# Chunk 0 of a delta-rule chain feeding a GELU MLP: masked Gram products from the plain Gram matrix, loads on two queues, a new order for the early part

## The chip, the cores and the metric

The kernel runs on one core of a Trainium2 chip. The metric is the device time of one execution in microseconds; runs of one kernel are summed up by their median. The profile is one further execution, recorded instruction by instruction.

## What is computed

The reference runs a delta-rule recurrence per batch and head (4 x 8 heads, 768 tokens, 48 numbers a head), lays the heads of a token side by side (3072 tokens x 384), and puts the result through an MLP with 2048 hidden features:

```python
k_n = k / (np.linalg.norm(k, axis=-1, keepdims=True) + 1e-06)
for t in range(S):
    y[:, :, t] = q_t @ state
    state = state + beta_t * outer(k_n_t, v_t - k_n_t @ state)
x = y.transpose(0, 2, 1, 3).reshape(B * S, H * D)
h = x @ w_in                                   # 384 -> 2048
out = gelu_tanh(h) @ w_out                     # 2048 -> 384
```

## The kernel before

The sequence is cut into 12 chunks of 64 tokens (`c` = 0 to 11). A chunk has two units (`u = 2c + x`) of 8 head slots on 128 partitions. All steps are added as named operations, and one text, `ORDER`, lists them in the order in which each engine takes them: `name:a` is ScalarE (ACT), `:d` VectorE (DVE), `:g` GpSimd (POOL), `:s` SyncE (SP), a name without a letter is TensorE (PE), and `@n` is the PSUM bank. Semaphore waits come from the reads and writes of the operations. Each engine works through its own list strictly in order, and a load is an entry of the list of the queue that issues it.

For each chunk the steps are these.

- `k c.ay`, `q`, `v`: loads of 96 KB each (chunk 0's keys in eight quarters `k0x0`, `k0x1` of 48 KB), into three slots a tensor. `sq`, `sum`, `pow`, `eps`, `inv`, `kn`: the keys are normalised; `qb`, `vb` convert queries and values.
- `T` or `Tk`, `Tq`, then `kT`, `kTk`, `kTq`: transposes on PE and the copies out of PSUM. `G` or `GD`, `GQ`: Gram matrices, copied by `dn` (keys with keys) and `wq` (keys with queries).
- The leaf: `F` gathers the 8 x 8 diagonal blocks, `lp`, `x0`, `L` and six pairs `xm`, `xa` on DVE solve them row by row; `xb` multiplies by beta and `xe` spreads the result into the block-diagonal tile `zt`.
- `KZ` multiplies the keys by `zt` on PE, `kz` copies the negative out as the third part of `kT`, and `GM` forms from it the products of the remaining inverse, which `lw` writes under a mask into the tile `lw`. `X10`, `X11` build the start, `A4`, `rt4`, `B4`, `bde4` (or `xi4`, `bdc4`), `A5`, `rt5`, `B5`, `be5` double the inverted blocks to 64.
- The chain: `V`, `K`, `R`, `U`, `Un`, `S`, `Sn` carry the state; `Q`, `O`, `On` give the chunk's output; `X` and `xT` transpose it on PE (or `turnx` by a DMA transpose).
- The MLP: sixteen `up` of three matmuls, four `gelu` on ACT, eight `down` of four matmuls, and copies and stores `Z`, `out`.

The two halves of the first weight matrix (`w1.0`, `w1.1`, 768 KB each) are issued by POOL. They are declared as readers of the slot of chunk 1's keys, so that they start after those keys:

```python
A(("pool",), f"w1.{i}", lambda e, P, f0=f0: e.dma_start(W1[:, :, f0:f0 + FF // 2], w1v[:, :, f0:f0 + FF // 2]),
  reads=["kraw10", "kraw11"], writes=[f"W1{i}"], dma=f"w1{i}")
```

The keys of chunk 4 go into that slot, so every `k4` load waits until both halves have landed. `w2` and the slot of chunk 0's values stand in the same way, and hold back `v3`.

`fill` operations are matmuls of a zero tile `wz` (128 x 128 by 128 x 512) that nothing reads; 140 are declared and the order of before uses two.

Of the kernel before, what the change touches and what calls it, by code (L numbers as in the profile page):

```python
# [8 lines left out]
ALU = mybir.AluOpType  # L9
# [3 lines left out]
C = 64  # L13
# [16 lines left out]
mwp1:g dn.5:a GM.1@4 xec.1:d KZ.0@0 ladj5.0:a F.2@3 wqa.5:a betaC3:a lw.1:d kz.0:a lp.2:d bdz1:d L.2@3 k3.01:s GM.0@4 x0.2:d X10.1:g KZ.2@6 lw.0:d  # L30
KZ.3@0 kz.3:a X11.1:g kz.2:a xm1.2:d GM.3@0 xa1.2:d rpad1:g A4.1@2 X11.0:g lw.3:d X10.0:g rt4.1:d k3.10:s xm2.2:d A4.0@1 X11.3:g xa2.2:d v1.01:s
B4.1@2 xm3.2:d xa3.2:d rt4.0:d q3.11:s GQ.2@6 GM.2@4 vb.0:a xm4.2:d vb.1:g wq.2:d k4.11:s B4.0@1 bde40.1:a triwq3:g lw.2:d V.0@6 X10.3:g k4.01:s
bde41.1:a bde40.0:a k4.00:s wqb.1:g xa4.2:d A4.3@2 xm5.2:d bde41.0:a A5.1@0 k4.10:s rt4.3:d GQ.3@4 R.0:a rt5.1:d A5.0@1 X11.2:g B4.3@2 v1.10:s rt5.0:d
B5.1@0 bde40.3:a xa5.2:d q3.00:s B5.0@7 X10.2:g xm6.2:d fill115@1 xa6.2:d be50.1:d be50.0:a v1.11:s wq.3:d xb.2:g be51.1:a A4.2@3 sq.3:a w2.0:g
be51.0:d v2.01:s xe.4:d U.0@0 bde41.3:d KZ.4@4 Un.0:a w2.1:g rt4.2:d kz.4:a O.0@6 sum.3:d A5.3@4 On.0:a S.0@2 rt5.3:d GM.4@0 sq.4:a xe.5:d X.0@6
B4.2@7 lw.4:d Sn.0:a fill85@4 KZ.5@4 xT.0:a sum.4:d X11.4:g bde40.2:a up4.0@2 kz.5:d pow.3:g up0.0@0 bde41.2:a up1.0 X10.4:d tabG:a up2.0 up12.0@6
qbc.3:d up3.0 A5.2@4 up13.0 rt5.2:d gelu0.0:a up5.0 up6.0 GM.5@4 eps.3:d inv.3:d knc.3:d up7.0 up14.0 A4.4@0 lw.5:d up15.0 turn.7:s B5.2@1 gelu3.0:a
rt4.4:d up8.0@4 X11.5:g up9.0 gelu1.0:a B5.3@0 vbc.1:g down00.0@6 be50.3:d up10.0 be51.3:a X10.5:d pow.4:g be50.2:a up11.0 V.1@2 gelu2.0:a T.6@0
v2.00:s A4.5@7 kT.6:d v2.10:s be51.2:a K.1 down01.0 R.1:a rt4.5:d q5.00:s G.6@4 k5.10:s B4.5@7 dn.6:a B4.4@2 xi4.5:d U.1@0 bde40.4:a down02.0 k5.00:s
wq.6:d bdc40.5:g Un.1:a down03.0 k5.01:s bde41.4:d bdc41.5:g eps.4:g A5.5@1 k5.11:s Z0.0:d wqb.5:g S.1@4 Q.1@2 q4.11:s Sn.1:d G.7@6 O.1 vbc.2:g  # L40
q4.01:s A5.4@0 rt5.5:d On.1:a down10.0@5 inv.4:d q4.10:s dn.7:d kn.9:g down11.0 rt5.4:d q4.00:s wq.7:d F.3@1 q5.01:s B5.4@4 lp.3:d V.2@2 sq.5:a x0.3:d
# [73 lines left out]
class Flow:  # L115
# [74 lines left out]
    def emit(self, nc, psum):  # L190
        count, total, names = {e: 0 for e in self.queues}, {}, list(self.queues)
        for e in self.queues:
            for o in self.queues[e]:
                if o.dma is None:
                    count[e] += 1
                    o.tag = (e, count[e])
                else:
                    if o.dma not in total:
                        total[o.dma] = 0
                        names.append(o.dma)  # L200
                    total[o.dma] += 16
                    o.tag = (o.dma, total[o.dma])
# [56 lines left out]
def bass_deltanet__then__act_gelu_tanh_kernel(  # L259
# [16 lines left out]
    LB = 8  # L276
# [627 lines left out]
```

## Time and profile before

| what | value |
|---|---|
| median of 3 runs | 255.12 us (253.94 to 255.86) |
| profiled execution, first to last instruction | 254.7 us |
| time of the profiled execution outside its span | not given by the page; the median is 0.42 us above the span |
| TensorE busy | 226.0 us, 89% |
| VectorE busy | 185.8 us, 73% |
| ScalarE busy | 157.4 us, 62% |
| GpSimd busy | 130.1 us, 51% |

Shares of busy time are taken over the whole span; the part before the first `up` and the part after it differ, so the profile is read stage by stage. In a row of a group or of a timeline, the line number is that of the operation or of a helper that records it (L343 and L349 are the copy and the negation that many steps use). In the table by stretches, each engine has its busy time in us and the number of its instructions, then come the granted TensorE clock (1.00 is full), the mean share of the DMA engines and GB/s.

### The profile page before, as it was taken

Reading aid. Unit: us, or ns where it says so; the run is one execution under the profiler, and the core shown is the slowest. Engines: PE = TensorE matmul, PEld = TensorE weight load, DVE = VectorE, ACT = ScalarE, POOL = GpSimd, SP = SyncE. Lnnn points to the kernel's source line nnn. Section 1 sums busy time; section 2 is a strip of 40 time slices with the busy share of each in tenths; the row PEclk is TensorE's granted clock in tenths of the full one; section 3 lists DMA queues with packets and bytes.
Section 4 is the critical chain, followed back from the end, with each engine's and each line's share of the span. In section 5 each row is a group of like instructions: output and inputs, shape, how many; then the busy total and the mean of one; then the engine's idle time right before and its main releaser. Section 6 shows DMA issues by size and latency. Waiting matters only on the chain.

```text
span 254.7 us, 12256 instructions
## 1 busy us (share of the span) xinstructions
PE 226.0 (89%) x5500; PEld 178.3 (70%) x5502; DVE 185.8 (73%) x445; ACT 157.4 (62%) x244; POOL 130.1 (51%) x159
## 2 busy tenths in 40 slices
PE   0259558899999998999999899999999999999994
PEld 0148347687877877777778778787786778678672
DVE  6599989955996989898888779898494665755100
ACT  2637747949568888967647577743866534436261
POOL 7647448347563397627358968472535525330000
PEclk9999956689999999999999999999999999999999
DMA  5986995987785679789678517787359320332042
GB/s 103 165 144 118 184 162 95 165 127 117 128 130 105 112 126 124 135 165 147 119 146 167 100 36 131 147 153 130 56 93 167 62 49 4 33 68 64 3 93 62
DMA packets 104532, 28.25 MB, mean 111 GB/s; under 512 B 98592, under 2 KB 103712, under 8 KB 104480
## 3 DMA queue, kind: packets, MB, share of 16 engines
q1 hardware_dynamic: 99200, 23.79, 54.0%
q0 software_dynamic: 2880, 3.15, 7.8%
q8 instruction: 43, 0.70, 1.2%
q10 hardware_dynamic: 2400, 0.54, 1.1%
q14 instruction: 9, 0.07, 0.1%
HBM read 20.64 MB, written 4.72 MB: 100 GB/s over the span
## 4 chain that ended last, share of the span: by engine, by line
PE 73%; DVE 15%; ACT 4%; DMA 2%; ACTq 2%; issue 2%; SPq 1%; POOL 0%
PE ps L835 24%; PE ps L824 22%; PE ps L692 5%; PE ps L620 3%; PE ps L752 3%; PE ps L773 2%; DMA vraw<-in_v_dram 2%; PE ps L697 2%; PE ps L564 2%; DVE lw L623 2%; DVE xl L658 2%; PE ps L633 2%; PE ps L759 2%; DVE ps L655 2%; PE ps L609 1%
## 5 line engine op out<-in xcount | busy, mean ns | idle before, releaser
L824 PE MATMUL ps<-xT,W 128*128 128x256 bf16 x576 | 76.8, 277 | 0.4 <-DVE xl L658 0.4
L835 PE MATMUL ps<-W,gT 128*128 128x384 bf16 x384 | 72.7, 326 | 0.0
L828 ACT ACTIVATE gT<-ps 128x1024 bf16<-128x1024 f32 x48 | 48.4, 1022 | 26.4 <-PE ps L824 25.8
L824 PEld LDWEIGHTS ps<-xT,W 128*128 128x128 bf16 x576 | 52.2, 99 | 9.3 <-DVE xl L658 0.5
L835 PEld LDWEIGHTS ps<-W,gT 128*128 128x128 bf16 x384 | 34.0, 97 | 18.2
L682 POOL TENSOR_SCALAR_AFFINE_SELECT bd<-lw 64x512 bf16<-64x512 bf16 x34 | 22.6, 667 | 37.7 <-DVE lw L623 28.6
L704 DVE TENSOR_TENSOR rl<-ps,two 128x384 bf16<-128x384 f32 (+1 forms) x48 | 22.9, 484 | 9.7 <-PE ps L692 9.5
L623 DVE CAST_PREDICATED lw<-mlw,ps 128x832 bf16<-128x832 uint16 x24 | 24.3, 1018 | 6.8 <-PE ps L620 6.5
L499 POOL TENSOR_TENSOR nrm<-nrm,half 128x16 f32<-128x16 f32 x9 | 26.6, 2956 | 2.8 <-DVE nrm L497 2.7
L343 ACT ACTIVATE bd<-ps 32x256 bf16<-32x256 f32 (+1 forms) x40 | 16.8, 428 | 8.2 <-PE ps L692 4.4
L692 PEld LDWEIGHTS ps<-lw,bd 128*128 128x128 bf16 x384 | 15.5, 98 | 4.2 <-POOL bd L682 1.2
L692 PE MATMUL ps<-lw,bd 128*128 128x32 bf16 (+1 forms) x384 | 17.2, 183 | 1.2 <-POOL bd L682 1.1
L658 DVE TENSOR_TENSOR xl<-ps,xl 128x96 bf16<-128x96 f32 (+4 forms) x72 | 16.0, 228 | 2.0
L655 DVE TENSOR_TENSOR ps<-ps,xl 128x64 f32<-128x64 f32 (+5 forms) x72 | 15.6, 221 | 2.0 <-PE ps L649 0.5
L343 ACT ACTIVATE ob<-ps 128x384 f32<-128x384 f32 x17 | 8.3, 490 | 14.0 <-PE ps L835 14.0
L722 POOL COPY bd<-xi 64x256 f32<-64x256 f32 x20 | 8.0, 401 | 16.4 <-ACT xi L343 8.5
L540 PE MATMUL ps<-ident,tok 128*128 128x128 bf16 x80 | 7.8, 246 | 8.1 <-POOL tok L531 3.8
L531 POOL TENSOR_TENSOR tok<-kraw,nrm 128x384 bf16<-128x384 f32 x9 | 8.5, 945 | 12.7 <-DVE bsb L349 5.6
L349 ACT ACTIVATE kT<-ps 128x512 bf16<-128x512 f32 x18 | 10.4, 596 | 6.4 <-PE ps L609 6.4
L343 ACT ACTIVATE dn<-ps 128x512 bf16<-128x512 f32 x18 | 10.4, 593 | 5.3 <-PE ps L564 5.3
L620 PE MATMUL ps<-kT 48*64 48x56 bf16 (+1 forms) x768 | 11.1, 196 | 2.8 <-ACT kT L349 1.4
L599 POOL TENSOR_TENSOR zt<-xb,blk 128x2048 bf16<-128x2048 bf16 x3 | 10.9, 3642 | 4.1 <-DVE xb L669 3.9
(132 smaller groups left out, 428.3 us busy)
## 6 DMA issues: line engine op xcount, KB each, us to landing
qraw<-in_q_dram SPq DMA_DIRECT2D x48, 96.0 KB, 3.6
vraw<-in_v_dram SPq DMA_DIRECT2D x48, 96.0 KB, 3.5
kraw<-in_k_dram SPq DMA_DIRECT2D x44, 96.0 KB, 3.6
out_dram<-ob SPq DMA_DIRECT2D x22, 192.0 KB, 3.0
W<-in_moe_w_in_dram POOLq DMA_DIRECT2D x2, 768.0 KB, 8.8
W<-in_moe_w_out_dram POOLq DMA_DIRECT2D x2, 768.0 KB, 9.6
kraw<-in_k_dram ACTq DMA_DIRECT2D x7, 48.0 KB, 3.3
out_dram<-ob SPq DMA_DIRECT2D x3, 96.0 KB, 2.2
```

The costliest lines, as they stand in the source:

```text
L343: return e.activation(out, in_, ACT.Copy) if e is nc.scalar else e.tensor_copy(out, in_)
L499: if e is nc.scalar else e.tensor_tensor(nr[:, 1, hx], nr[:, 0, hx], half[:, hx], ALU.pow), reads=[nrn, "half"] + ["one"] * (c < ROOTS),
L620: ins = e.matmul(P(ps("GM"))[hf(a), o_ + c0:o_ + c1], kT[s][r, y, g, hf(a)], kT[s][r, z, g, C * a + c0:C * a + c1])
L623: A(("dve",), op("lw"), lambda e, P: e.copy_predicated(lw[m][:, :, 0:LW - LB], mlw[:, :, :].rearrange("p w t -> p (w t)")[:, 16:16 + LW - ...
L655: A(("dve",), f"xm{m}.{c}", lambda e, P, m=m, w=w, part=part: e.tensor_tensor(part(P), P(f"L.{c}")[:, off[m]:off[m] + 2 * H * w].rearrange ...
L658: A(("dve",), f"xa{m}.{c}", lambda e, P, m=m, part=part: e.tensor_tensor(xl[y][:, :, m + 1:LB], part(P), xl[y][:, :, m + 1:LB], ALU.add), ...
L682: A(("pool", "dve"), op(f"X1{a}"), lambda e, P, src=lw[m][hf(a), :, LW - C:LW], dst=bd[b_][hf(a), :, hf(a)], a=a: e.affine_select(out=dst, ...
L692: ins = e.matmul(P(name)[:, C * h + c0:C * h + c1], bd[b_][:, h, :], rhs[:, h, :])
L704: A(("dve",), op(f"rt{i}"), lambda e, P, i=i, c0=c0, c1=c1, r_=r_: e.tensor_tensor(r_[:, 0:H, c0:c1], P(ps(f"A{i}")).rearrange("p (h t) -> ...
L824: ins = e.matmul(P(ph)[:, 256 * f:256 * f + 256].rearrange("p (x t) -> p x t", x=2), W1[:, j, 128 * (i + f):128 * (i + f) + 128], x_[:, :, ...
L828: A(("act",), f"gelu{i // 4}.{c}", lambda e, P, i=i, ph=ph: e.activation(g_[:, i:i + 4, :], P(ph).rearrange("p (f t) -> p f t", f=4), ACT. ...
L835: ins = e.matmul(P(po)[:, 0:DM], g_[:, f, 128 * b:128 * b + 128], W2[:, f, :], start=(f == 0), stop=(f == FC - 1))
```

## The change

Four things are changed; what the kernel computes stays the same.

1. For chunk 0 alone, `KZ` and `kz` go. `GM` is formed straight from `dn`, the Gram matrix that is copied anyway, and `zt`. The sign that `kz` gave is put into `xb.0`, and taken out again where `R.0` copies.
2. Every load may be issued from SP or ACT. ACT issues 25 of them instead of 7, all before the unchanged part of its list; the stores may go on either queue, and in the text all but one (`out01.11`) stay on SP, as before.
3. Semaphore counts of DMAs are given in the order of the text rather than queue by queue, since one tensor's loads may now be issued from two queues.
4. `ORDER` is new up to the middle of chunk 1's MLP. From `up3.1` on PE (and from `qb.11` on DVE, `gelu0.1` on ACT, `pow.5` on POOL, `turn.9` on SP) each engine's list is that of before, with other PSUM banks.

Up to `up3.1` PE's list loses `KZ.0`, `KZ.1` and `X.1` (chunk 1 is transposed by `turnx.1`, a DMA, instead) and has 37 fills in place of two. The fills come in runs of one to six between the early steps. `GM.4`, `B4.2` and `KZ.5` stood ahead of the first `up` and now stand behind it; the first `up` is now `up8.0` instead of `up4.0`. `On.0` goes from ACT to DVE, `X10.1`, `X11.1`, `X10.0` from POOL to DVE, `dn.2` and `dn.3` from ACT to DVE. On ACT the words around one load are now

```
wqa.1:a q3.01:a q5.11:a kz.3:a dn.5:a vbc.0:a dn.4:a wqa.4:a wqa.5:a k4.11:a kz.2:a bde40.1:a bde41.1:a triwq3:a xi4.0:a R.0:a
```

and POOL's list around the weights is `kn.0 trilw0 triwq1 rpad0 sq.2 mln0 mwp0 w1.0 mln1 eps.2 triwq2 pad5 mwp1 qb.4 w1.1`.

The diff without the order text:

```diff
-        for e in self.queues:
-            for o in self.queues[e]:
-                if o.dma is None:
-                    count[e] += 1
-                    o.tag = (e, count[e])
...
+        for o in self.queue:
+            if o.dma is None:
+                count[o.on] += 1
+                o.tag = (o.on, count[o.on])
...
-                            A(("sp", "act") if c == 0 and n == "k" else SP, f"{n}{c}" + ("" if x is None else f"x{x}") + f".{a}{y}",
+                            A(("sp", "act"), f"{n}{c}" + ("" if x is None else f"x{x}") + f".{a}{y}",
...
+            def direct(e, P):
+                for g in range(4):
+                    for p, a in quad:
+                        h, o_ = 4 * p + g, 512 * p + 2 * C * g
+                        e.matmul(P(ps("GM"))[hf(a), o_ + LW - C:o_ + LW - LB], zt[m][hf(a), h, hf(a)], d_[hf(a), h, 0:C - LB])
+                        ins = e.matmul(P(ps("GM"))[hf(a), o_:o_ + C - 16], d_[hf(a), h, :], zt[m][hf(a), h, C * a + 16:C * a + C])
+                return ins
+            if not c:
+                d_ = dn[0][:, H * x:H * x + H, :]
+                A(PE, op("GM"), direct, reads=[f"dn0{x}", f"zt{m}"], alloc=(ps("GM"), 2), mode="t", mm=32)
+            else:
... (keys, KZ, kz and gram as before)
-            A(("dve", "pool"), f"xb.{c}", lambda e, P: e.tensor_tensor(xb[y][:, :, :], xl[y][:, :, :], bc[:, c, :, :], ALU.mult),
+            A(("dve",) if c == 0 else ("dve", "pool"), f"xb.{c}", lambda e, P: e.scalar_tensor_tensor(xb[y][:, :, :], xl[y][:, :, :], -1.0, bc[:, c, :, :], op0=ALU.mult, op1=ALU.mult) if c == 0 else
+              e.tensor_tensor(xb[y][:, :, :], xl[y][:, :, :], bc[:, c, :, :], ALU.mult),
...
-            A(EV, op("R"), lambda e, P: copy(e, rb[...], banks(P(ps("K")))), frees=[ps("K")], writes=[rbn])
+            A(EV, op("R"), lambda e, P: (neg if first else copy)(e, rb[...], banks(P(ps("K")))), frees=[ps("K")], writes=[rbn])
...
-                        A(SP, f"out{a}{a}.{c}", lambda e, P, a=a, o_=o_: e.dma_start(
+                        A(("sp", "act"), f"out{a}{a}.{c}", lambda e, P, a=a, o_=o_: e.dma_start(
```

212 lines of the change are left out of this document (107 added, 105 removed).

## The prediction

> **What bounds the kernel now.** I read the page first, for the span and the shape over time, and then cut the span into stages with the table by stretches.
>
> ```profile
> span 254.7 us, 12256 instructions
> PEclk9999956689999999999999999999999999999999
> ```
>
> ```profile
> 0.00:15.00 15.00, 2.06 (x16) 1.70 (x16) 9.66 (x27) 6.53 (x11) 11.14 (x33) 1.00 0.78 136
> 15.00:44.65 29.65, 21.10 (x606) 17.97 (x607) 27.69 (x86) 18.92 (x36) 16.34 (x28) 0.83 0.82 140
> 44.65:49.94 5.29, 4.26 (x167) 3.68 (x168) 5.27 (x8) 5.03 (x8) 1.53 (x3) 0.68 1.11 160
> 49.94:75.45 25.51, 25.29 (x613) 20.19 (x606) 19.30 (x44) 16.68 (x26) 15.86 (x14) 0.93 0.84 132
> 75.45:254.70 179.25, 173.28 (x4109) 134.73 (x4107) 123.92 (x283) 110.18 (x166) 85.23 (x84) 1.00 0.56 99
> ```
>
> PE is the bound from the first `up` at 49.94 to the end: 25.29 of 25.51 us, then 173.28 of 179.25. The last row is the part whose lists are kept, from the end of `up3.1`. Before the MLP it is DVE: 27.69 of 29.65 us from 15.00 to 44.65, where its last early step, `be51.0`, releases `U.0`. So the change can move two things: when the first `up` starts, and what PE needs from there to `up3.1`. What follows shifts as a block. The chain of waits shows the link between the two stages, and the PEclk line shows a half clock just there.
>
> ```profile
> 44.22 0.43 DVE bd L343
> 45.30 0.81 ACT us L343
> 50.01 3.74 PE ps L824 x18
> 53.94 0.99 PE ps L824 x9
> 54.93 0.37 PE ps L620 x32
> 56.06 0.20 PE ps L692 x8
> ```
>
> The first six `up` take 3.74 us for 18 matmuls, the next three 0.99 for 9.
>
> **Term 1, DVE ahead of U.0.** The removed Gram step (`KZ`, `kz`) stands on PE and ACT, beside a DVE that has other work. What counts is DVE's list up to the step that releases `U.0`; both texts have 111 entries there. The groups up to 50 us and two lines of the timeline give the prices.
>
> ```profile
> L602 DVE TENSOR_TENSOR zt<-xb,blk 128x1024 bf16<-128x1024 bf16 x4 | 2.7, 702 | 0.1
> L571 DVE CAST_PREDICATED wq<-muq,ps 128x512 bf16<-128x512 uint16 x4 | 2.7, 674 | 0.0
> L343 DVE COPY kT<-ps 128x512 bf16<-128x512 bf16 x6 | 2.3, 416 | 0.3 <-PE ps L540 0.2
> L421 DVE MEMSET bd<- 128x512 f32 x4 | 1.9, 485 | 1.1 <-PEq L889 1.0
> L599 DVE TENSOR_TENSOR zt<-xb,blk 128x2048 bf16<-128x2048 bf16 x1 | 1.2, 1210 | 0.0
> L418 DVE TENSOR_SCALAR rl<-tmpl 128x256 bf16<-128x256 bf16 x1 | 0.9, 904 | 0.0
> L343 DVE CAST bd<-ps 32x256 bf16<-32x256 f32 x2 | 0.8, 410 | 0.0
> L658 DVE TENSOR_TENSOR xl<-ps,xl 128x48 bf16<-128x48 f32 x3 | 0.7, 225 | 0.0
> L346 DVE TENSOR_SCALAR bd<-ps,low 128x512 bf16<-128x512 f32 x1 | 0.7, 746 | 0.0
> ```
>
> ```profile
> 13.06 1.96 DVE L531 TENSOR_TENSOR tok<-kraw,nrm 128x384 bf16<-128x384 f32 x1
> 14.95 0.54 DVE L531 TENSOR_TENSOR tok<-kraw,nrm 128x384 bf16<-128x384 f32 x1
> 12.63 2.05 POOL L382 TENSOR_SCALAR_AFFINE_SELECT rows<-rows 128x1024 bf16<-128x1024 bf16 x1
> ```
>
> Gone from the list: `xec.1` 1.21, `wq.3` and `wq.4` 1.35, two `kTk` 0.83, two presets (`trilw0`, `triwq1`, priced as the memset of 485 ns) 1.0, `ladj5.1` and `ladj4.1` 0.9, `be50.1` and `be51.0` 0.82, five leaf steps of chunk 1's successor 1.0 (0.2 each), and some six small ones 0.8: 7.9 us. New: `xe.3` 0.70, `dn.2` and `dn.3` 1.4 (nearest row: 0.746 for 512 numbers out of PSUM), three `X1` 1.2 (0.41 as the casts of half width), `kn.1` and `sq.0b` 1.1 (0.54 each), `kTq.2` and `be51.1` 0.83, two memsets, `trilw1` and `triwq0` 2.0, `ladj5.0` 0.45, `qb.1`, `bdc40.0` and four small ones 1.1: 8.8 us. Balance +0.9. Against it stands one stall. `kn.2` took 1.96 us beside POOL's 2.05 us `rows1`, its twin 0.54; `rows1` now stands before any `kn`, so 1.4 us go. Term 1 is -0.5 us, if DVE waits as long as before (5.3 us up to 15.00, 2.0 after).
>
> That is the unknown. No row shows the waits of the new order. Below, the 5.3 us could halve, since chunk 0's keys are now issued first: -2.7. Above, new waits appear. `betaN000` and `qb.1` are placed on DVE behind loads that are the tenth on ACT and the twentieth on SP, and `xe.3` waits for a POOL `xb.1`. I allow +2. I take zero, by this row:
>
> ```profile
> 10.00:20.00 10.00, 4.74 (x90) 3.80 (x91) 9.01 (x24) 4.87 (x11) 5.11 (x9) 1.00 0.86 152
> L472 SPq DMA_DIRECT2D kraw<-in_k_dram x13: 634/637/2834, 0.8 to 25.6; - x13
> ```
>
> The DMA engines were 0.86 busy with 152 GB/s, and one queue at 96 KB per 0.64 us offers 150. A second queue can reorder the data, but hardly bring more of it. The Trainium skill says as much in "DMA: Bandwidth & Descriptors", section "Issuing engines are not separate DMA queues": loads from several engines run on the same 16 DMA engines, and only the issue time is saved. The trace agrees (0.86 at 152 GB/s); by it, the second queue alone would be worth nothing, and the sum would be the same. On ACT each issue costs about 0.6 us of its list, and twelve stand among steps that others wait for; I count them inside the +2.
>
> **Term 2, from U.0 to the first up.** Before, 5.29 us. In the rows below, `KZ.5` waited 0.36 us for DVE ahead of the first `up`; it moves behind it: -0.35. `X.0` at half clock took 0.82 us, a later `X` at full 0.50: -0.3. `U.0` shrinks alike: -0.1. `On.0` goes from ACT to DVE, behind `sum.3`; ACT took 0.81 for 768 numbers (its `Un` in the chain), DVE 0.746 for 512: +0.2. Term 2 is -0.55, bounds -1 and +1. The first `up` comes at 48.9.
>
> ```profile
> 49.58 0.43 PE L609 MATMUL ps<-zt,tok 64*64 64x64 bf16 x16 [0.36 <-DVE lw L623]
> 47.97 0.82 PE L807 MATMUL ps<-ident,xo 128*128 128x128 bf16 x6
> 68.50 0.50 PE L807 MATMUL ps<-ident,xo 128*128 128x128 bf16 x6
> 33.00:43.00 10.00, 7.53 (x255) 6.78 (x256) 8.97 (x24) 5.20 (x10) 7.29 (x12) 0.50 0.68 117
> 30.00:34.00 4.00, 1.74 (x78) 1.42 (x78) 3.94 (x7) 2.85 (x6) 0.29 (x1) 0.86 1.29 189
> 46.60:53.50 6.90, 6.49 (x123) 5.24 (x122) 4.95 (x8) 5.51 (x9) 3.61 (x2) 0.51 1.27 193
> ```
>
> **Term 3, the clock.** PE ran at half from 33 to 43 us and from 46.6 to 53.5. It fell after a stretch with 1.74 of 4 us busy. From 30 us on the new text puts 19 fills among the early steps. A fill streams 512 columns; at the `up` rate of 0.11 us for 256 (0.99 / 9) one is 0.22 us at full clock, so they add 4.2 us in some 18, a quarter of the time. I take the clock as full at the first `up`: 3.74 becomes 1.98, -1.75. If it is not, zero; below zero nothing, as the 18 matmuls then take what they took. The fills' price ahead of the MLP is hidden by PE's idle time (8.55 us of 29.65); placed in front of a step that others wait for, one costs 0.22 to 0.42, inside the +2 above. The Trainium skill, "TensorE: Matmul & The Clock Gate", section "What's actually happening", lets the clock fall after an idle window of about 3.4 us. Here it fell with PE 43% busy, so sparse work is enough; by the page alone the fills would have nothing to prevent, and the term would be the same only because the half clock was measured.
>
> **Term 4, PE from the first up to up3.1.** Three groups now stand behind the first `up`: `GM.4` 0.37, `B4.2` 0.20 and `KZ.5`, as half of the 0.43 at half clock, 0.22. Two fills add 0.44. `X.1` goes, 0.4. Together +0.85. `turnx.1` replaces `X.1`: three `down` and ten short groups, some 4 to 5 us of PE work, stand between `O.1` and `up12.1`, and a transpose lands 3.5 us after its issue behind a 0.81 us `On`; no stall is charged; if that cover is gone, each us late is a us.
>
> ```profile
> xT<-xo SPq DMA_TRANSPOSE x8, 3.5
> ```
>
> **Sum.** -0.5 - 0.55 - 1.75 + 0.85 = -1.95, so a span of 252.75. The median of before lies 0.42 above its profiled span; with the same 0.42 the forecast is **253.2 us**, 0.75% below 255.12. The runs of before themselves spread over 1.92 us, so a change within 1% (252.6 to 257.7) can hardly be told from none.
>
> **The rivals.** *The early part really shortens.* If half of DVE's 5.3 us of early waits go and nothing new appears, `U.0` comes 2.7 us sooner: 250.5. For it: the keys of chunk 0 were late before (one quarter was issued at 9.6 us on ACT), and DVE's 9.66 of 15 us leaves room. Against: DVE stays at 27.69 of 29.65 afterwards, with more work on its list.
>
> *ACT is held by the weights: slower.* `k4.11` now stands in ACT's list, and it must wait until both halves of W1 have landed. Before, SP paid for that:
>
> ```profile
> 23.45 1.01 POOL L481 DMA_DIRECT2D W<-in_moe_w_in_dram  x1
> 29.16 0.81 POOL L481 DMA_DIRECT2D W<-in_moe_w_in_dram  x1
> 38.11 3.40 SPq L472 DMA_DIRECT2D kraw<-in_k_dram  x4
> SPq L472 <- DMA W<-in_moe_w_in_dram: 5.9, 1, 5.9
> DMA to landing us min/median/max: 7.9/8.8/11.3
> 38.96 0.59 ACT L343 ACTIVATE bd<-ps 64x512 bf16<-64x512 f32 x1 [2.24 <-PE ps L692]
> ```
>
> SP stood 5.9 us and issued the first `k4` at 38.11, 8.95 us after the second half. Behind `k4.11` on ACT are `kz.2`, for which `GM.2` and with it `V.0` and `B4.0` wait, then `bde40.1`, for which `A5.1` waits: the path to `U.0`. `bde40.1` ran at 38.96; with the issue and `kz.2` (0.6 each) ahead, `k4.11` is free up to about 37.2. POOL issued the halves at 23.45 and 29.16; now eight short entries stand between them, so I put the first at 21.5 to 23 and the second at 25 to 26. It lands at 34 to 35 (8.8 us), or 37.3 at the longest landing seen. Both halves and the loads of two queues now compete: 1.57 MB and six loads of 96 KB make 2.2 MB, which from 21.5 on take until 37.7 at the 136 GB/s of the first 15 us, and until 43.7 at the last stretch's 99. The forecast's gain of 1.95 is eaten when the weights land after 39.2. At 41 the hold is 3.8 us, and PE idles into the half clock as before, so the 1.75 goes too: 253.2 + 3.8 + 1.75 = 258.7.
>
> *The clock stays at half.* The fills sit in bunches and run through at once, so the gaps between remain: 253.2 + 1.75 = 255.0, no change.
>
> **Chances.** Forecast 0.42, early part shorter 0.30, ACT held 0.14, half clock 0.14. Faster by over 1%: 0.27 of the second and 0.13 of the first's lower edge, 0.40. Slower by over 1%: ACT held in its worse half and a little from stacked waits, 0.12. Within 1%: 0.48. The range goes from below the second case to the middle of the third, 250.0 to 257.2.
>
> **What would show it.** In the profile after: the first `up` at 48.9 and its first 18 matmuls in about 2 us; PEclk without the 5 and 6 digits; DVE near 5.3 us idle up to 15; ACT without a wait for W ahead of `kz.2`; the stretch from `up3.1` to the end still near 179 us. The prediction is wrong if that last stretch changes, since then the block did not shift whole, or if DVE's waits moved by more than 2 us.

## The result: 0.9% slower, where 0.75% faster was forecast

| kernel | median, us | runs | ratio to before, 95% interval |
|---|---|---|---|
| before | 254.33 (253.07 to 257.08) | 20 | |
| after | 256.81 (255.90 to 259.88) | 20 | 1.0093 [1.0068, 1.0118] |

The change costs 2.5 us. Within these two samples single executions lie up to 4 us apart; the ratios leave the disturbed ones out. In the runs below a timed execution is 1.7 to 1.9 us longer than its span (the profiled one of after: 256.19 us, span 254.5), so the profiled execution of before with its span of 254.7 took 256.4 us or a little more. It was a long one of its kernel.

The page of after, and the table by stretches, cut at the start of `U.0`, at the first `up` and at the end of `up3.1` as before (per engine busy us and instructions in the order PE, PE weight loads, DVE, ACT, POOL, then clock, DMA share, GB/s):

```profile
span 254.5 us, 12234 instructions
PEclk9998999999999999999999999999999999999999
```

```profile
0.00:15.00 15.00, 3.87 (x36) 2.52 (x37) 10.96 (x35) 5.02 (x9) 9.59 (x28) 1.00 1.02 144
15.00:44.13 29.13, 23.48 (x564) 17.14 (x573) 25.34 (x79) 17.36 (x34) 17.58 (x25) 0.94 1.05 159
44.13:48.86 4.73, 3.25 (x127) 2.65 (x129) 4.62 (x12) 3.62 (x6) 4.53 (x6) 1.00 1.07 146
48.86:74.69 25.83, 24.95 (x660) 19.55 (x658) 21.23 (x42) 18.59 (x29) 17.12 (x20) 1.00 0.74 109
74.69:254.50 179.81, 174.47 (x4110) 134.38 (x4107) 124.35 (x285) 109.97 (x165) 87.79 (x84) 1.00 0.55 101
```

Up to the first `up` this is what was forecast: the clock line has no 5 or 6, and the first `up` starts at 48.86 (forecast 48.9). The stretch to `up3.1` is longer than forecast (25.83 us against 25.51 - 1.75 + 0.85 = 24.6), and the last one, which was to stay at 179.25, has 0.56 us more, with the same 4110 matmuls. To see more, the span of before had to be put right first: the kernel before, unchanged, profiled once more.

```profile
span 251.6 us, 12256 instructions
PEclk9999756799999999999999999999999999999999
```

```profile
0.00:15.00 15.00, 3.50 (x28) 2.81 (x28) 9.81 (x30) 6.72 (x12) 10.97 (x32) 1.00 1.06 133
15.00:43.18 28.18, 20.77 (x597) 17.61 (x596) 25.97 (x83) 18.64 (x36) 17.54 (x30) 0.76 1.02 147
43.18:48.30 5.12, 4.13 (x166) 3.56 (x168) 5.12 (x8) 4.98 (x8) 1.35 (x3) 0.74 1.06 144
48.30:73.43 25.13, 24.01 (x613) 19.45 (x606) 19.76 (x46) 16.64 (x26) 16.08 (x14) 0.99 0.93 141
73.43:251.60 178.17, 173.14 (x4109) 134.61 (x4107) 123.38 (x282) 110.26 (x166) 85.50 (x83) 1.00 0.56 100
```

The same program is 3.1 us shorter: 1.6 before the first `up`, 0.4 to `up3.1`, 1.1 behind. It has as much half clock as the shown execution, 17.1 us by the clock records of both traces, but in other places: from 28.5 to 42.2 and from 45.6 to 49.0 us, where the shown one has 32.9 to 43.2 and 46.6 to 53.4. So its half clock ends 0.7 us into the MLP, and its first eighteen `up` take 2.47 us instead of 3.81 (PE's timeline of before, then of before_again):

```profile
49.94 3.81 PE L824 MATMUL ps<-xT,W 128*128 128x256 bf16 x18
48.30 2.47 PE L824 MATMUL ps<-xT,W 128*128 128x256 bf16 x18
```

Against this execution the changed kernel is 0.6 us later at the first `up` and loses 0.7 and 1.6 us in the last two stretches. One execution doesn't settle a stage; the table collects those profiled in the experiments below (us, from the same three marks, read from PE's timeline). Line numbers in rows shift a little from kernel to kernel with the text above them.

| kernel | `U.0` | first `up` | first `up` to `up3.1` | rest | span |
|---|---|---|---|---|---|
| before, as shown | 44.70 | 49.94 | 25.51 | 179.25 | 254.7 |
| before_again | 43.18 | 48.30 | 25.13 | 178.17 | 251.6 |
| before_renamed | 44.71 | 50.56 | 25.16 | 177.58 | 253.3 |
| before_fills | 44.80 | 49.86 | 23.86 | 178.58 | 252.3 |
| before_banks | 44.80 | 49.78 | 24.52 | 180.50 | 254.8 |
| after | 44.13 | 48.86 | 25.83 | 179.81 | 254.5 |
| after_leaf | 44.75 | 49.76 | 27.62 | 179.62 | 257.0 |
| after_banks | 44.53 | 49.34 | 25.60 | 178.66 | 253.6 |
| after_banks_q0 | 44.90 | 50.29 | 27.74 | 178.57 | 256.6 |
| after_banks_x1 | 43.93 | 48.60 | 26.03 | 178.27 | 252.9 |
| hybrid_early_after | 44.29 | 49.47 | 27.74 | 177.59 | 254.8 |
| hybrid_q0 | 44.35 | 49.40 | 25.81 | 178.69 | 253.9 |

### The profile page after: what moved, and what is told of

Same layout as the page of the kernel before. It is cut to its first block, busy times and chain, and to the rows that moved or that the text cites. A ratio compares the mean times of both kernels' runs of the same rounds, so it can differ in the third digit from the quotient of the medians.

```text
span 254.5 us, 12234 instructions
## 1 busy us (share of the span) xinstructions
PE 230.0 (90%) x5488; PEld 176.2 (69%) x5499; DVE 186.5 (73%) x448; ACT 154.6 (61%) x242; POOL 136.6 (54%) x160
## 4 chain that ended last, share of the span: by engine, by line
PE 70%; DVE 13%; SPq 5%; POOL 3%; ACT 3%; DMA 2%; issue 2%; DVEq 0%
PE ps L848 24%; PE ps L837 22%; PE ps L705 5%; SPq L473 4%; PE ps L765 2%; DMA qraw<-in_q_dram 2%; PE ps L612 2%; PE ps L565 2%; PE ps L710 2%; ACT gT L841 2%; PE ps L772 2%; PE ps L645 2%; PE ps L786 2%; PE ps L628 1%; DVE lw L635 1%
## 5 line engine op out<-in xcount | busy, mean ns | idle before, releaser
L837 PE MATMUL ps<-xT,W 128*128 128x256 bf16 x576 | 75.2, 273 | 0.5 <-ACT gT L841 0.5
L695 POOL TENSOR_SCALAR_AFFINE_SELECT bd<-lw 64x512 bf16<-64x512 bf16 x31 | 20.7, 672 | 27.6 <-DVE lw L635 23.3
L705 PE MATMUL ps<-lw,bd 128*128 128x48 bf16 (+1 forms) x384 | 16.8, 180 | 1.6 <-DVE bd L697 0.5
L603 POOL TENSOR_TENSOR zt<-xb,blk 128x1024 bf16<-128x1024 bf16 x7 | 13.8, 1984 | 4.5 <-DVE xb L682 4.3
L670 DVE TENSOR_TENSOR xl<-ps,xl 128x96 bf16<-128x96 f32 (+3 forms) x66 | 14.7, 227 | 1.7
L667 DVE TENSOR_TENSOR ps<-ps,xl 128x96 f32<-128x96 f32 (+5 forms) x66 | 14.4, 221 | 2.1 <-PE ps L661 0.4
L350 ACT ACTIVATE kT<-ps 128x512 bf16<-128x512 f32 x16 | 9.3, 596 | 7.5 <-PE ps L628 7.5
L532 POOL TENSOR_TENSOR tok<-kraw,nrm 128x384 bf16<-128x384 f32 x7 | 7.2, 1032 | 11.4 <-DVE nrm L504 6.4
L587 POOL TENSOR_TENSOR wq<-wq,muq 128x512 bf16<-128x512 bf16 x11 | 12.8, 1171 | 0.4
L344 DVE CAST bd<-ps 32x256 bf16<-32x256 f32 (+1 forms) x21 | 8.8, 422 | 5.3 <-ACT bd L344 3.1
```

The lines of the kernel that those rows point to most:

```text
L344: return e.activation(out, in_, ACT.Copy) if e is nc.scalar else e.tensor_copy(out, in_)
L603: A(("dve", "pool"), op("xe"), lambda e, P: e.tensor_tensor(zt[m][:, :, :].rearrange("p h (b j) -> p h b j", j=LB), xb[y][:, H * x:H * x + ...
L667: A(("dve",), f"xm{m}.{c}", lambda e, P, m=m, w=w, part=part: e.tensor_tensor(part(P), P(f"L.{c}")[:, off[m]:off[m] + 2 * H * w].rearrange ...
L670: A(("dve",), f"xa{m}.{c}", lambda e, P, m=m, part=part: e.tensor_tensor(xl[y][:, :, m + 1:LB], part(P), xl[y][:, :, m + 1:LB], ALU.add), ...
L695: A(("pool", "dve"), op(f"X1{a}"), lambda e, P, src=lw[m][hf(a), :, LW - C:LW], dst=bd[b_][hf(a), :, hf(a)], a=a: e.affine_select(out=dst, ...
L705: ins = e.matmul(P(name)[:, C * h + c0:C * h + c1], bd[b_][:, h, :], rhs[:, h, :])
```

## The experiments

Theories at the start: the shown execution of before was longer than the usual one, and with it the clock's term too large; the second queue costs; the direct products cost. Later ones came from the traces. Each ratio is to runs of before on the same chip, taken alongside.

### The base and the clock

**before_again**: no edit.

> The kernel before, unchanged, for its own executions. Clock theory: the profiled execution that the prediction was made from (span 254.7, clock 0.966) was one in which PE fell to half clock ahead of the first up; an ordinary one shows a clock of 0.98 to 1.00, a span near 252.5 and the first up before 49.5 with 18 matmuls in about 2 us, so term 3 had nothing to gain. Rival (the profile was typical): the new profile again shows about 0.966 and a span near 254.7, and the loss must come from elsewhere.

Measured 254.11 us, 1.0011 [0.9984, 1.0037]. The profile is the second one above. Neither theory holds whole: the clock is as low as in the shown execution (0.964 on the mean, where that one had 0.966), but the span, the first `up` and the eighteen matmuls come out near the first theory. Of the 3.1 us between the two executions, the place of the half clock makes 1.3.

**after_nofill**: the changed kernel without its fills.

```diff
-... fill100@2 ... fill48@3 ... fill62@3 ... fill76@4
+(every fill word removed)
```

> The changed kernel without its 37 fills. Clock theory: PE falls to half clock in some executions, the first 18 up take up to 3.7 us instead of 2; the median is 0.5 to 1.8 us slower than the changed kernel and the runs spread more. Rival (fills stand in the way of early steps and the clock holds anyway): up to 1 us faster than 256.8.

Measured 260.65 us, 1.0281 [1.025, 1.0311], 3.8 us above after. The stretch 28 to 48 us of after_nofill and of after, from the table by stretches of each:

```profile
28.00:48.00 20.00, 14.17 (x386) 12.27 (x386) 17.73 (x47) 12.54 (x22) 11.43 (x13) 0.63 0.79 135
```

```profile
28.00:48.00 20.00, 15.82 (x486) 11.58 (x491) 18.69 (x48) 13.47 (x24) 12.70 (x15) 1.00 0.89 147
```

Without fills the clock is 0.63, PE gets through 386 matmuls instead of 486, and `U.0` starts at 46.34 instead of 44.13. In the changed order the fills are worth their place.

**before_fills**: 17 fills in the order of before, in the bank of the step behind them.

```diff
+one fill ahead of T.4, Tq.2, G.5, F.2, L.2, U.0, O.0, KZ.5; two ahead of KZ.1, GM.1, GM.3; three ahead of A4.0
```

> The order of before, with 17 single matmuls of 512 columns added in PE's gaps between about 22 and 48 us, nothing else. Theory A (the clock of the early part is worth time by itself, in any order): the first up comes 1 to 3 us sooner, its first 18 matmuls take 2.0 us, the whole 1.5 to 3.5 us faster than before, near 251.5. Theory B (before the MLP the list on DVE sets the pace; the clock matters only in the 18 matmuls): 0.3 to 0.7 us faster. Theory C (a fill that stands in front of a step on the path costs its 0.22 to 0.43 us): up to 2 us slower.

Measured 255.76 us, 1.0054 [1.0023, 1.0086]: slower. Its clock line is the proof that the edit did its work:

```profile
span 252.3 us, 12283 instructions
PEclk9999999999999999999999999999999999999999
```

The clock is full throughout, the first eighteen `up` take 2.14 us, and the stretch from the first `up` to `up3.1` is the shortest of the table, but `U.0` does not come sooner (44.80). The table by stretches of before_fills has for it:

```profile
49.86:73.72 23.86, 23.31 (x605) 18.97 (x606) 18.83 (x43) 16.64 (x26) 15.38 (x14) 1.00 0.82 139
```

In the order of before the early part is paced by DVE, as the prediction had read, and not by PE's clock. The profiled execution was the fastest of eleven (254.19 us), so it does not show where the median's 1.4 us go.

### The queues

**after_sp**: the changed order, with the loads that it gives to ACT issued by SP.

```diff
-k2.10:a v2.10:a q1.10:a q2.10:a ...
+k2.10:s v2.10:s q1.10:s q2.10:s ...
```

> The changed kernel with all loads that the change put on ACT put back on SP, in the same text order. Data theory (two queues make the loads of chunk 0's queries land late and DVE waits 1.8 us for them, and ACT loses its issue time): 1 to 2 us faster than the changed kernel, 254.8 to 255.8. Rival (the order itself costs the time, or the loads are needed from two queues): 256.8 or slower, since SP at 0.65 us an issue delivers the queries still later.

Measured 262.82 us, 1.035 [1.0309, 1.0392]: 6.0 us above after. In its profile (span 264.4 us) `U.0` starts at 50.27 instead of 44.13, so the loss lies in the early part. The second queue is no loss; in this order it is worth more than any other part that was undone.

**after_banks_q0** and **hybrid_q0**: one load moved. The timeline of DVE in after shows why:

```profile
20.71 0.36 DVE L344 CAST tok<-qraw 128x384 bf16<-128x384 f32 x1 [1.83 <-DMA qraw<-in_q_dram]
```

```diff
-k2.11:s ... q0.01:s ... q1.11:s q2.00:s ... q0.10:s
+q0.10:s k2.11:s ... q0.01:s ... q1.11:s q2.00:s
```

> after_banks (the changed kernel with before's banks from U.2 on, 256.29) with one load moved: q0.10 is issued ahead of k2.11 on SP instead of five loads later. In the changed kernel DVE waited 1.83 us for it at 20.7 (issued 14.46, landed 6.23 later). Theory A (the early part is DVE's list, and this wait is in it): 1.0 to 1.8 us faster than after_banks, 254.5 to 255.3. Theory B (the DMA engines are full between 10 and 20 us, so another load is late in its place): the same within 0.5 us.

> hybrid_early_after (the changed early part, before's text from T.6 on, 255.8) with the same load moved. Theory A (the wait for q0.10 is in the path): 1.0 to 1.8 us faster, 254.0 to 254.8, level with before. Theory B (the DMA engines are full): the same as hybrid_early_after within 0.5 us.

Measured 255.95 us, 1.0088 [1.0045, 1.0132], where after_banks had 1.0052 [1.0023, 1.0082]; and 255.33 us, 1.0014 [0.998, 1.0047], where hybrid_early_after had 1.0039 [1.0006, 1.0072]. The wait for `q0.10` is gone from both traces, but `U.0` stays at 44.90 and 44.35, and neither pair of intervals is apart. Why the 1.83 us do not show is not settled. Both traces have a stop of PE ahead of `U.0` that the two kernels without the move do not have, in the middle of a step and with nothing to wait for; PE's timeline of after_banks_q0, then of hybrid_q0:

```profile
33.40 0.44 PE L565 MATMUL ps<-kT 48*64 48x64 bf16 x18 [1.43 <-issue]
32.82 0.44 PE L565 MATMUL ps<-kT 48*64 48x64 bf16 x18 [1.15 <-issue]
```

Either the wait was taken up by later waits, or such a stop took its place. More of these stops come below.

### The direct products

**before_direct**: before's order, chunk 0's products direct; `KZ.0`, `kz.0`, `KZ.1`, `kz.1` left out, and chunk 0's `dn` in the third `gelu` buffer, which is filled only later.

```diff
-KZ.1@4 kz.1:a ... KZ.0@0 ... kz.0:a
+A(PE, op("GM"), direct, reads=[f"dn2{x}", f"zt{m}"], ...)
```

> The kernel before with the direct Gram products of chunk 0 alone (the Gram copy of chunk 0 has a buffer of its own), same order, without KZ.0, KZ.1 and their copies. DVE theory (term 1 of the prediction: what bounds the early part is DVE's list, which is not shortened): same as before, within 0.5 us of 254.3. Rival (the removed step was on the path): 1 to 1.5 us faster.

Measured 258.94 us, 1.0181 [1.0155, 1.0206]: 4.6 us slower, which neither theory gave.

**after_gram**: the reverse, the changed kernel with `KZ` and `kz` put back directly ahead of `GM`.

```diff
-GM.1@4 ... GM.0@6
+KZ.1@4 kz.1:a GM.1@4 ... KZ.0@6 kz.0:a GM.0@6
```

> The changed order, queues and fills, but chunk 0's Gram products as in before: KZ.0, kz.0 (on ACT), KZ.1 and kz.1 stand directly ahead of GM.0 and GM.1, with the positive sign of before. Theory A (the direct products cost time of their own, 4.6 us in before's order): faster than the changed kernel by 2 us or more, 254.5 or less. Theory B (they save the steps in the path, KZ 0.3 us, kz 0.6 us and two handovers): slower than the changed kernel by 0.5 to 2 us, 257.3 to 259.

Measured 260.06 us, 1.0252 [1.0223, 1.0282], 3.2 us above after; in its profile `U.0` starts at 46.33 instead of 44.13. So in the new order the direct products save, although `KZ` had no better place than the one directly ahead of its reader.

**before_direct_fills**: before_direct with the 17 fills (the two of `KZ.1` ahead of `GM.0`).

> The order of before with chunk 0's masked Gram products direct, as in before_direct (1.018 of before), and the same 17 fills. Theory A (the direct products cost because PE has less work in the early part and sits at half clock longer): the two kernels with fills come out alike within 0.7 us. Theory B (the direct products cost something of their own, a code load on PE or a longer step): this one stays 3 to 5 us behind before_fills. Theory C (noise of one build): anything between.

Measured 257.82 us, 1.0144 [1.0113, 1.0175]: 2.1 us behind before_fills. This run does not take the clock out, since here the fills did not hold it: it is at half from 33.0 to 43.2 us. PE stood 2.04 us ahead of a fill, DVE's `lw.0` then waited 2.19 us for `GM.0`, and `U.0` starts at 47.88 instead of 44.80. From the page of before_direct_fills, PE's timeline and DVE's:

```profile
PEclk9999956999999999999999999999999999999999
33.58 0.61 PE L426 MATMUL ps<-wz 128*128 128x512 bf16 x1 [2.04 <-DVE lp L649]
36.38 1.02 DVE L635 CAST_PREDICATED lw<-mlw,ps 128x832 bf16<-128x832 uint16 x1 [2.19 <-PE ps L619]
```

That the clock is not what makes before_direct slower is read from two other traces: half clock lasts 17.1 us in before_direct and 17.1 us in before. In before_direct PE stood ahead of `L.2` with `GM.0` queued behind it:

```profile
32.56 0.47 PE L660 MATMUL ps<-lp,rows 128*128 128x96 bf16 x6 [2.00 <-DVE lp L648]
```

**direct_gm0** moves `GM.0` in front of it, **direct_gm0_lw** also DVE's readers.

```diff
-GM.1@4 xec.1:d ... F.2@3 ... lw.1:d lp.2:d ... L.2@3 ... GM.0@4 ... lw.0:d
+GM.1@4 GM.0@0 xec.1:d ... F.2@3 ... lw.1:d lp.2:d ... L.2@3 ... lw.0:d     (direct_gm0)
+GM.1@4 GM.0@0 lw.1:d lw.0:d xec.1:d ... F.2@3 ... lp.2:d ... L.2@3         (direct_gm0_lw)
```

> before_direct (before's order, chunk 0's Gram products direct, 258.94) with GM.0 moved on PE from behind L.2 to directly behind GM.1, in the bank that KZ.0 had. In before_direct PE stood 2.00 us at L.2 for lp.2, with GM.0 queued behind it though its operands were there, and the clock fell to half. Theory A (direct products cost in before's order only because GM.0 keeps the place that it had behind L.2): 1.5 to 3 us faster than before_direct, 256 to 257.4. Theory B (the direct products cost something of their own): the same as before_direct within 0.7 us.

> direct_gm0 with DVE's lw.1 and lw.0 moved ahead of xec.1 (1.21 us), so that DVE takes the direct products as soon as they are there. Theory A (the direct products save their steps when both lists follow them): faster than before by 0.5 to 2 us, 252.5 to 254. Theory B (DVE's list has the same length, only its order changes): as direct_gm0 within 0.7 us. Theory C (xec.1 comes too late for KZ.2 and KZ.3): 1 us slower than direct_gm0.

Measured 260.09 us, 1.0192 [1.0149, 1.0235], and 259.60 us, 1.0186 [1.0146, 1.0227]: as before_direct. The place of `GM.0` is not the cause either. What the traces do show is a stop of PE that no wait explains. From PE's timeline of before_direct, then of direct_gm0:

```profile
95.54 0.35 PE L627 MATMUL ps<-zt,tok 64*64 64x64 bf16 x21 [1.56 <-issue]
...
104.29 0.41 PE L764 MATMUL ps<-st,kT 48*64 48x48 bf16 x28 [0.52 <-issue]
```

```profile
100.13 0.35 PE L627 MATMUL ps<-zt,tok 64*64 64x64 bf16 x21 [1.77 <-issue]
...
109.70 0.41 PE L764 MATMUL ps<-st,kT 48*64 48x48 bf16 x28 [1.08 <-issue]
```

Both stop inside a step, with 21 of its 32 matmuls left, and again with 28 of 32 left; direct_gm0_lw stops at the same two places (1.18 and 0.57 us). In before_renamed that part of PE's timeline has no such stop. But stops inside a step are in all twenty profiles, at other places, those with before's own text included (the last section says where). Their sum is 3.7 us in before_direct's profile and 0.5 to 2.1 us in the five profiles of the table with before's early text. With the stops taken off, the rest of before_direct is 177.7 us, as short as theirs. So they make about 2.5 of the 3.0 us by which its span (256.0) is above the mean of before, before_again, before_renamed and before_fills (253.0). That profiled execution, 257.87 us, was 1.1 below the median of its kernel; what the median has besides, and why this kernel meets more stops, no run shows.

### The part behind the first MLP block

**after_leaf**: chunk 3's leaf off POOL. In after, POOL's `xe.6` (1.92 us) stands ahead of `pow.5` on its list, and DVE waits for that; POOL's and then DVE's timeline:

```profile
72.14 1.92 POOL L603 TENSOR_TENSOR zt<-xb,blk 128x1024 bf16<-128x1024 bf16 x1
74.01 2.94 POOL L500 TENSOR_TENSOR nrm<-nrm,half 128x16 f32<-128x16 f32 x1
```

```profile
76.98 0.18 DVE L502 TENSOR_SCALAR nrm<-nrm 128x16 f32<-128x16 f32 x1 [1.87 <-POOL nrm L500]
```

```diff
-ym1.3:g ym4.3:g ya4.3:g ya5.3:g ya6.3:g xb.3:g xe.6:g sum.5:d ... pow.5:g ... xe.7:d
+ym1.3:d ym4.3:d ya4.3:d ya5.3:d sum.5:d ya6.3:d pow.5:g xb.3:d xec.3:d
```

> The changed kernel with chunk 3's leaf kept off POOL: its five POOL steps, xb.3 and xe.6 (1.92 us on POOL) go to DVE, xe.6 and xe.7 as one xec.3, and pow.5 comes directly behind sum.5, as in before. Theory A (the loss behind up3.1 is POOL's delay of pow.5, kn.10 and T.10, which leaves DVE and ACT late for the next 50 us): the rest after up3.1 falls from 179.8 to about 178.5, the whole 0.8 to 1.6 us faster than the changed kernel, near 255.4. Theory B (DVE is the late engine there, and POOL relieves it): 0.5 to 2 us slower than the changed kernel. Theory C (POOL's delay is taken up by later waits anyway): the same within 0.5 us.

Measured 255.99 us, 1.0094 [1.0062, 1.0126]: as after. The delay of `pow.5` is not what the change lost.

**after_banks**: what was left was something that isn't in the lists. Each engine's list behind `up3.1` is the same word for word, but 204 of its 244 bank numbers differ, and 93 takings follow another earlier holder. PE's timeline of after shows the result:

```profile
93.58 0.50 PE L837 MATMUL ps<-xT,W 128*128 128x256 bf16 x3 [0.49 <-ACT gT L841]
107.20 0.41 PE L705 MATMUL ps<-rl,bd 128*128 128x64 bf16 x8 [0.23 <-DVE wq L572]
124.88 0.44 PE L795 MATMUL ps<-us,tok 64*64 64x48 bf16 x32 [0.30 <-ACT gT L841]
```

The first is `up4.2`: it takes a bank that `gelu0.2` is still reading, where in before it follows `B5.7`. The edit gives the takings from `U.2` on the banks of before, renamed so that they fit.

> The changed kernel, with one thing undone: from U.2 on, each PE step takes the PSUM bank that it has in before (up to a renaming of the eight banks). No list of an engine changes. In the changed kernel 93 of the 244 bank takings behind up3.1 follow another earlier holder than in before; PE waited 0.49 us for a gelu at 93.6 us and 0.30 at 124.9, where before shows no such wait. Theory A (the part behind up3.1 is longer because PE waits for banks that were filled last): that part falls from 179.8 to 178.2 to 178.8, the whole 1.0 to 1.6 us faster than the changed kernel, near 255.3. Theory B (it is longer because POOL delays pow.5 and kn.10, and DVE and ACT are late): the same as the changed kernel within 0.4 us, 256.4 to 256.8.

**before_banks**: the reverse edit in before.

> The kernel before, with the changed kernel's PSUM banks from U.2 on (eight of some 250 takings apart, which had to be placed otherwise). No list changes. Theory A (banks): 1.0 to 1.6 us slower than before, 255.2 to 255.8. Theory B (POOL's delay): the same as before within 0.4 us.

**before_renamed**, the control: before with its banks renamed as wholes.

> A control for the bank runs: the kernel before with its eight PSUM banks renamed as wholes (0 to 6, 2 to 2, 4 to 0, 6 to 4), so that every taking follows the same holder. Theory A (who held the bank before is what costs): the same as before within 0.3%, 253.7 to 255.2. Theory B (any edit of the banks, or any new build, moves the time by as much): 1 to 2 us off before, as before_banks (256.55) was.

Measured: after_banks 256.29 us, 1.0052 [1.0023, 1.0082]; before_banks 256.55 us, 1.0072 [1.0045, 1.0100]; before_renamed 254.67 us, 1.0008 [0.9981, 1.0035]. The waits go and come with the banks. PE's timeline of before_banks, where before_again has none for `gT`:

```profile
75.50 0.45 PE L608 MATMUL ps<-zt,tok 64*64 64x64 bf16 x32 [0.46 <-ACT gT L827]
92.92 0.50 PE L823 MATMUL ps<-xT,W 128*128 128x256 bf16 x3 [0.49 <-ACT gT L827]
...
124.63 0.44 PE L781 MATMUL ps<-us,tok 64*64 64x48 bf16 x32 [0.30 <-ACT gT L827]
```

Of the kernels looked at for it, the six with the changed banks (after, after_leaf, after_gram, before_banks, hybrid_late_after, and after_nofill) have a rest of 179.3 to 181.8 us; the nine with those of before, without direct products in before's order, have 177.6 to 179.3. Part of this spread is the stops, 0 to 1.8 us of a rest here. With them taken off, the rest is 178.9 to 180.4 us in the seven profiles with the changed banks (those six and after_sp) and 177.2 to 178.7 in the thirteen others, direct products included. So it is shown that the banks cost time: 1.8 us in before's order by the ratio. In the changed kernel the rest falls by 1.2 us when they are undone, and the ratio by 0.4%, 1.0 us, but there the two intervals overlap.

The waits for `gT` are not the whole of it. They are 0.79 us in after and none in after_banks, but after_banks has other waits, so that PE's idle time in the rest falls only from 5.34 to 5.04 us. The larger part of the 1.2 us is PE's busy time, 174.47 against 173.62 us with the same 4110 matmuls, and how the banks make PE's steps longer no run shows.

**hybrid_early_after** and **hybrid_late_after**: the two texts cut at `T.6`, behind chunk 0's `up` steps, and joined crosswise.

```diff
 changed text up to T.6
-A4.5@2 ... turnx.1:s ... Lc.3:a ym1.3:g ... xe.6:g ... fill62@3 ... fill76@4 ...   (changed text)
+... X.1@6 ... xm1.3:d ... xT.1:d ... xec.3:d ...   (before's text and banks)
```

> The changed order (with queues, fills and direct products) up to T.6, behind the ups of chunk 0; from there on before's text, with its banks, X.1 on PE and chunk 3's leaf on DVE. Theory A (the early part of the change is worth nothing or less, and the loss lies behind chunk 0's ups): 2.0 to 2.9 us faster than the changed kernel, 253.9 to 254.8, the same as before. Theory B (the loss lies in the early part): 256.3 to 256.8, as the changed kernel.

> The reverse: before's order up to T.6, and from there on the changed text (turnx.1, chunk 3's leaf partly on POOL, two fills, its banks up to seven takings), loads on SP. Theory A (the loss lies behind chunk 0's ups): 1.5 to 2.9 us slower than before, 255.6 to 257.0. Theory B (the loss lies in the early part): the same as before within 0.5 us.

Measured 255.80 us, 1.0039 [1.0006, 1.0072], and 259.71 us, 1.0188 [1.015, 1.0226]. The changed early part, with its queues, fills and direct products, comes out 0.4% above before; the changed text behind it costs 4.8 us by the ratio when it stands behind the early part of before, for which it was not made.

**after_banks_x1**: after_banks with `X.1` back on PE, without fills 62 and 76.

```diff
-turnx.1:s ... fill62@3 ... fill76@4
+X.1@6 K.2 ya2.3:d xT.1:d
```

> after_banks with X.1 on PE and xT.1 on DVE in place of the transposing DMA turnx.1, and without the two fills behind chunk 0's ups (62 and 76). Theory A (the stretch from chunk 0's ups to up3.1, 17.7 us in after_banks and 16.8 in an ordinary run of before, is longer because of these edits): 0.5 to 1.0 us faster than after_banks, 255.3 to 255.8. Theory B (they are covered): the same within 0.4 us.

Measured 256.94 us, 1.0076 [1.0042, 1.0110]: not faster than after_banks. The stretch to `up3.1` stays at 26.03 us, so neither `turnx.1` nor the two fills explain its length.

No version beats before; hybrid_q0 (1.0014) is level with it.

### What makes the stretch to `up3.1` jump

The table has 25.6 to 26.0 us for some kernels with the changed early text and 27.6 to 27.7 for others, which differ in something else. PE's timelines name the difference, first after_leaf, then after_banks_q0, then hybrid_early_after:

```profile
65.73 0.56 PE L705 MATMUL ps<-lw,bd 128*128 128x32 bf16 x16 [1.14 <-issue]
75.58 0.30 PE L795 MATMUL ps<-us,tok 64*64 64x48 bf16 x13 [0.64 <-issue]
...
66.27 0.56 PE L705 MATMUL ps<-lw,bd 128*128 128x32 bf16 x16 [1.14 <-issue]
76.06 0.30 PE L795 MATMUL ps<-us,tok 64*64 64x48 bf16 x13 [0.60 <-issue]
...
67.43 0.31 PE L565 MATMUL ps<-kT 48*64 48x128 bf16 x8 [1.06 <-issue]
```

These are the stops again, at the start of a step or inside it, 1.8, 1.7 and 1.1 us in sum; after_leaf and after_banks_q0 have them at the same instructions. The stretch of after has 0.39 us of them, that of after_banks none. In hybrid_early_after half clock also lies on the first `up`, from 49.7 to 53.1 us, and makes 1.5 us. With the stops taken off, and the clock (what the first eighteen `up` took beyond the time at full clock), the five kernels with before's early text need 23.3 to 23.7 us for the stretch, and the seven with the changed one 25.1 to 26.0. So the changed text costs 2.1 us there, of which a clock that happens to be at half in before hides up to 1.7.

## Why the prediction was wrong, step by step

Two steps failed outright: "What follows shifts as a block", and term 4, which put the new text's cost from the first `up` to `up3.1` at 0.85 us where it is 2.1. Term 3 and the base made the gain look larger than it is in most executions.

**The base.** "The median of before lies 0.42 above its profiled span; with the same 0.42": this failed. The time outside the span is 1.7 to 1.9 us, so the shown execution took at least 256.4 us, 2.1 above the median of the 20 runs. The sum of -1.95 with 1.7 gives 254.45, no change. That alone moves the forecast by 1.3 us, and means that the late start and late `up3.1` of the shown execution were partly that execution's own.

**Term 1 (-0.5).** The number is there against the shown execution: DVE's busy time up to `U.0` went from 37.35 to 36.30 us, its idle time from 7.30 to 7.83, `U.0` from 44.70 to 44.13. The stall beside `rows1` went as forecast (`kn.3` and `kn.2` take about 0.5 us each in after), but it is not in every execution of before: before_again has 0.55 and 0.86 us where the shown one has 1.96 and 0.54. Against the other executions nothing is left: `U.0` starts at a mean of 44.44 in the five rows of the table that have before's early text and of 44.41 in the seven that have the changed one. The bound of +2 for new waits did hold the 1.83 us for `q0.10`, at the load named for it. But the reason given for taking zero, that a second queue brings little more data, was wrong for this order: without it the kernel is 6.0 us slower. "DMA: Bandwidth & Descriptors" of the Trainium skill, section "Issuing engines are not separate DMA queues", says that issuing from several engines saves only the issue time, usually small; here the issue time on one queue was not small.

**Term 2 (-0.55).** `U.0` to the first `up` went from 5.24 to 4.73 us, -0.51. Right; over the same rows of the table the means are 5.25 and 4.98.

**Term 3 (-1.75).** The mechanism was right and the clock came out full, but the size was that of one execution. Against the 2.14 us of before_fills, the first eighteen `up` lost 1.67 us in the shown execution, 0.33 in before_again, 1.25 in before_renamed and 0.58 in before_banks: 1.0 on the average. In before_fills the gain is there in the stretch, but not in the median. In the changed order the fills are worth 3.8 us, 2.2 of them ahead of `U.0`, where the term didn't look; they bring back what that order loses without them. Whether PE or DVE paces the early part decides what PE's clock is worth there, and the change moved it.

**Term 4 (+0.85).** Too small. At full clock before_fills needs 23.86 us from the first `up` to `up3.1` with PE busy 23.31; after needs 25.83, and with clock and stops taken off all kernels the difference is 2.1. The trace of after has no records of its two fills in this stretch, so after_banks, with the same list, is the one to compare:

```profile
49.34:74.94 25.60, 25.40 (x662) 19.41 (x658) 21.32 (x42) 18.47 (x29) 17.24 (x20) 1.00 0.74 111
```

PE is busy 2.1 us longer than in before_fills. The moved groups were priced well: from start to start `GM.4` takes 0.38, `KZ.5` 0.25, `B4.2` 0.24, the two fills 0.55, and `X.1` no longer takes 0.43, together 1.0. What the sum put at nothing is that PE's other groups take longer in the new order: from start to start the `up` matmuls take 8.76 us in after_banks and 8.30 in before_fills, and other groups about 0.1 us more each. These 1.1 us no run took apart.

**"What follows shifts as a block."** This failed. The lists do shift whole, the PSUM banks do not: 93 of 244 takings follow another holder, and the rest is 1.2 us longer in the changed order and 1.6 in before's, stops taken off. The text named this stretch as what would make the prediction wrong.

**The rivals.** ACT was never held by the weights: POOL issued the halves at 19.83 and 24.02 us, earlier than put, `k4.11` left at 35.88, and no ACT wait names `W`. The early part was not shorter. The clock was not at half at the first `up`.

The table, stops and clock taken off where said, gives -0.3 at the first `up` (means of the five kernels with before's early text and of the seven with the changed one), +2.1 to `up3.1` by the new text, -1.0 there by the clock, and +1.2 to 1.6 for the rest: 2.0 to 2.4, near the 2.5 measured. These are single profiled executions, so the agreement is no proof. The profile of after alone is only 1.5 us above the mean span of before, before_again, before_renamed and before_fills, since its execution was 0.6 below the median. Open are the 1.4 us of before_fills, what before_direct's median has beyond the stops, and what meets how many stops.

## What to carry to other kernels

A list that keeps its order is not kept if its PSUM banks change: compare, for each taking, who held the bank before. Make a sum against an execution only after its own time, span and what lies outside, is set beside the median of many. A step that is left out can save time in one order and cost time in another: here the same edit saved 3.2 us in one and cost 4.6 in the other, only in part for a known reason. Before a difference in one stage is put down to an edit, look for stops and for half clock in that stage; here they made up to 2 us of it.

## What the runs showed of the hardware

PE can stop in the middle of a step with nothing to wait for. In before_direct, direct_gm0 and direct_gm0_lw the two stops are 254 or 255 matmuls and 254 weight loads apart; the table by stretches between the two in before_direct:

```profile
95.54:104.29 8.75, 8.04 (x255) 6.76 (x254) 7.44 (x12) 6.83 (x9) 6.20 (x9) 1.00 0.86 112
```

That is about 510 instructions, with 0.5 to 1.8 us lost at each end. Such places are the same in every kernel. Count PE's instructions from the first, two for a matmul with its weight load and one for each wait of PE's sequencer: the 53 stops of 0.15 us or more inside a step, in all twenty profiles, lie 194 to 196 instructions behind a multiple of 256, and so do six at the start of a step. Those inside a step sum up to 0.2 to 3.9 us in a profile, and 0.9 and 2.1 us in two executions of before. "Runtime: NRT & Kernel Launch" of the Trainium skill, section "Instruction fetch mechanics", has instructions streamed in blocks of 256 with a cost at each block that is mostly hidden; the places agree with such blocks, the 1.8 us does not agree with a hidden cost. That it is the fetch is inferred from the places, no run took it apart. An edit that removes 64 instructions early shifts every later block against the steps, which is one way in which it can move time far from itself.

The granted clock is 1.00 or 0.50 in all clock records of the twenty traces, and half clock ahead of a program's end comes in pieces of 3.4 us or a whole multiple of it (3.4, 6.8, 10.2, 13.7 and 17.1). Where such a piece ends differs from execution to execution, and so does what the first `up` pay. In the changed order without fills it was at 0.63 over 20 us in which PE was busy 14.17 (at half clock a matmul also counts as busy for longer), and it stayed at 1.00 where single matmuls of 512 columns filled the gaps (15.82 of 20).
